# A last output transfer in three parts on two queues, and a shorter general path, in an attention and two-MoE kernel

## The chip, the cores and the metric

The kernel runs on one core of a Trainium2 chip. The metric is the time of one execution on the device in microseconds (us). TensorE is called PE, its weight loads PEld, VectorE DVE, ScalarE ACT, GpSimd POOL and SyncE SP. A profile was taken of one execution.

## The reference

Three stages follow each other; the inputs are float32 (the capacity is an integer, and some weights reach the chip as raw 64-bit words).

```python
q_p, k_p = phi(q * s), phi(k * s)          # phi: exp(h - max h) / sqrt(128), h = x @ omega.T - |x|^2 / 2
attn = (q_p @ (k_p.T @ v)) / (q_p @ k_p.sum(2) + 1e-6)      # 2 x 8 heads, 576 tokens, 64 wide
x = attn as 1152 tokens x 512
g = h * tanh(softplus(h)), h = x @ w_in                     # 512 -> 2048
x = g @ w_out                                               # 2048 -> 512
logits = x @ w_gate                                         # 8 experts
expert, gate = argmax and its softmax weight, per token
# an expert takes tokens in order up to its capacity of 288, the rest give 0
out[i] = gate[i] * (relu(x[i] @ w1[expert]) @ w2[expert])   # 512 -> 1024 -> 512
```

## The kernel before

The kernel is one function, `performer_mish_moe`, in stages: attention in 8 pairs of heads (lines 166 to 420), the first MLP's input product and its activation (lines 428 to 590), and then the routing and the experts (lines 591 to 871). The products are made in three matmuls each (`mm3`, lines 64 to 68), from a high and a low part of both operands.

The 1152 tokens form 4 groups of 288 (`G`, `GT`), each of 3 blocks of 96 (`TT`). The expert stage is written for tokens that need two pairs of a group and an expert: group 0 with its most frequent expert `eA`, and, out of groups 1 to 3, the group `g1 + 1` with its most frequent expert `eB`. These indices are found on the chip and read into registers (lines 709 to 712). The whole output is set to zero by one transfer from `zero` (line 529, pieces of 128 float32, 512 bytes), and the two pairs' results are written over it.

The second pair ends the kernel (lines 845 to 870). For each of the four 128-wide blocks `d` of the output, PE sums over 8 blocks of the hidden layer (`ffn2`). The block is copied from PSUM to `yo`, transposed on PE in three blocks of 96 tokens (`turn`), multiplied by the token's weight into `o` (`weigh`, on DVE for t = 0 and 2, on ACT for t = 1), and written to `out`. The work on block d - 1 is put into the middle of block d's sum. When blocks 0 and 1 are in `o`, SP issues their transfer (line 861, columns 0 to 255); blocks 2 and 3 go out together at the end (line 870, columns 256 to 511). Both write the rows from `row = R["g1"] * GT + GT`, a register's value, through `rows` (lines 759 and 760). In the last block the copy to `yo` is made in three pieces, all on ACT (lines 864 to 866).

```python
for t in range(3):
    c = slice(t * TT, t * TT + TT)
    S.copy(out=yo[:, 3, c], in_=py[3][:, c])
for t in range(3):
    turn(pt[t], yo, t, 3)
    weigh(o, pt[t], R["wB"], t, slice(384, 512), t == 1)
nc.sync.dma_start(out=rows(row, half[1]), in_=o[:, :, half[1]])
```

The order of instructions on each engine around here is the order of the code (`manual_schedule`); the Tile framework adds the waits on semaphores. After the last transfer every engine reads `nrem`, the number of tokens that the two pairs leave over (line 871), and branches: if it is over zero, the general path (lines 883 to 925) computes the output of all groups and experts anew. It has one loop over the 4 groups, with 16 tiles of `w_out` written out in it and 4 matmuls for each (64 in all), and a loop over groups and experts with 32 + 24 matmuls written out in it. If nothing is left over, every engine jumps over its share of this code to the end of the program, where SP and the others pass their semaphores and a common barrier.

Of the kernel before, what the change touches and what calls it, by code (L numbers as in the profile page):

```python
# [9 lines left out]
F32 = mybir.dt.float32  # L10
# [5 lines left out]
AF = mybir.ActivationFunctionType  # L16
# [4 lines left out]
NT, DM, DFF = 1152, 512, 2048  # L21
E, F1 = 8, 1024
NPAIR = NB * NH // 2
NJ = DFF // 128
KT = DM // 128
G, GT = 4, 288
TT, NTT = 96, 12
# [5 lines left out]
def performer_mish_moe(  # L33
# [15 lines left out]
    nc = tc.nc  # L49
    T, V, S, P = nc.tensor, nc.vector, nc.scalar, nc.gpsimd  # L50
# [22 lines left out]
    ident = cs[:, 0:128]  # L73
# [12 lines left out]
    def bank(tag, name):  # L86
        return psum.tile([128, 512], F32, name=name, tag=tag, bufs={"pj": 3, "qt": 2}.get(tag, 1))
# [35 lines left out]
    def convert(kind, j):  # L123

        t = raw.pop((kind, j))
        if kind == "wi":
            f = fpool.tile([128, 512], F32, name="wif", tag="wif", bufs=2)
            yield from conv64(t, f)
            yield
            hi = fhl.tile([128, KT, 128], F32R, name="wih", tag="wih")  # L130
            lo = fhl.tile([128, KT, 128], F32R, name="wil", tag="wil")
            split_hi_lo(f, hi.rearrange("p a b -> p (a b)"), lo.rearrange("p a b -> p (a b)"), "act", "dve")
            win[j] = (hi, lo)
        else:
            wo[j] = ring(F32)
            yield from conv64(t, wo[j])
# [12 lines left out]
    def steps(*gens):  # L149

        for _ in range(4):
            advance(*gens)
# [13 lines left out]
    with ExitStack() as c2:  # L166
        a1 = c2.enter_context(tc.tile_pool(name="a1", bufs=1))
# [246 lines left out]
    def g(j, c):  # L414
        return gt[j // 2][:, j % 2, c]
# [9 lines left out]
    with tc.manual_schedule():  # L425
# [97 lines left out]
        for j in range(NJ):  # L523
# [4 lines left out]
            if j == 6:  # L528
                nc.sync.dma_start(
                    out=out.rearrange("(p t) d -> p (t d)", p=128).rearrange("p (c f) -> p c f", f=128),  # L530
                    in_=zero[:, None, :].to_broadcast([128, NT * DM // 128 // 128, 128]),
                )
            if j in (9, 13):
# [3 lines left out]
                o=convert("wo", j + 1) if j + 1 < NJ else iter(()),  # L537
# [79 lines left out]
        R = {}  # L617
# [136 lines left out]
        def ffn2(n, ps, h1, f, d):  # L754
            s = slice(d * 128, d * 128 + 128)
            c = chunk[n, 8 + f]
            mm3(ps[d][:, :GT], c[0][:, s], c[1][:, s], h1[:, 0, f, :], h1[:, 1, f, :], f == 0, f == 7)

        def rows(first, c):
            return out[ds(first, GT), c].rearrange("(t p) d -> p t d", p=TT)  # L760

        def turn(pt, yo, t, d):
            T.transpose(pt[:TT, d * 128 : d * 128 + 128], yo[:, d, t * TT : t * TT + TT], ident)

        def weigh(o, pt, w, t, c, act):
            if act:
                S.activation(out=o[:, t, c], in_=pt[:TT, c], func=AF.Copy, scale=w[:, t : t + 1])
            else:
                V.tensor_scalar(out=o[:, t, c], in0=pt[:TT, c], scalar1=w[:, t : t + 1], scalar2=None, op0=ALU.mult)
# [54 lines left out]
        py = [bank(t, "py2") for t in ("b0", "b1", "b2", "qt")]  # L824
# [5 lines left out]
        yo = h3.tile([128, KT, GT], F32, name="yo", tag="em0")  # L830
# [3 lines left out]
        o = y2.tile([TT, 3, DM], F32, name="o", tag="o")  # L834
        for f in range(8):
            ffn1(1, yt1, h1, f)
            expert_split(1, 8 + f, "act", "pool" if f % 2 else "dve")
            if f < 3:
                pt = bank("pj", "pt")
# [5 lines left out]
        py = [bank(t, "py2") for t in ("b0", "b1", "b2", "qt")]  # L845
        yo = h3.tile([128, KT, GT], F32, name="yo", tag="em2")
        pt = [bank("pj", "pt") for _ in range(3)]
        o = y2.tile([TT, 3, DM], F32, name="o", tag="o")
        half = (slice(0, 256), slice(256, 512))
        row = R["g1"] * GT + GT  # L850
        for d in range(KT):
            for f in range(8):
                ffn2(1, py, h1, f, d)
                if f == 3 and d > 0:
                    for t in range(3):
                        turn(pt[t], yo, t, d - 1)
                    if d > 1:
                        for t in range(3):
                            weigh(o, pt[t], R["wB"], t, half[0] if d == 2 else slice(256, 384), t == 1)
                    if d == 2:  # L860
                        nc.sync.dma_start(out=rows(row, half[0]), in_=o[:, :, half[0]])
            if d < 3:
                (S.copy if d % 2 else V.tensor_copy)(out=yo[:, d, :], in_=py[d][:, :GT])
        for t in range(3):
            c = slice(t * TT, t * TT + TT)
            S.copy(out=yo[:, 3, c], in_=py[3][:, c])
        for t in range(3):
            turn(pt[t], yo, t, 3)
            weigh(o, pt[t], R["wB"], t, slice(384, 512), t == 1)
        nc.sync.dma_start(out=rows(row, half[1]), in_=o[:, :, half[1]])  # L870
        R["nrem"] = nc.values_load(R["ri"][0:1, 3:4], min_val=0, max_val=NT, skip_runtime_bounds_check_because="a count of tokens")
    y1.release()
    whB.release()
# [9 lines left out]
    with tc.If(R["nrem"] > 0):  # L883
        with ExitStack() as c2:
            q1 = c2.enter_context(tc.tile_pool(name="q1", bufs=1))
            q2 = c2.enter_context(tc.tile_pool(name="q2", bufs=2))
            yg = q1.tile([128, G, KT, GT], F32, name="yg")
            ob = q1.tile([TT, NTT, DM], F32, name="ob")
            V.memset(ob, 0.0)
            with tc.For_i(0, G, 1) as gi:  # L890
                ps = [bank(t, "pq") for t in ("pj", "b0", "b1", "b2")]
                for j in range(NJ):
                    t = q2.tile([128, 512], I64, name="wo64", tag="wo64")
                    nc.sync.dma_start(out=t, in_=w_out[j])
                    f = q2.tile([128, 512], F32, name="wof", tag="wof")
                    steps(conv64(t, f))
                    for d in range(KT):
                        T.matmul(out=ps[d][:, :GT], lhsT=f[:, d * 128 : d * 128 + 128], rhs=g(j, ds(gi * GT, GT)), start=(j == 0), stop=(j == NJ - 1))
                for d in range(KT):
                    V.tensor_copy(out=yg[:, ds(gi, 1), d, :].rearrange("p o t -> p (o t)"), in_=ps[d][:, :GT])  # L900
            with tc.For_i(0, G, 1) as gi:
                with tc.For_i(0, E, 1) as ei:
                    n = nc.values_load(R["cnti"][0:1, ds(gi * E + ei, 1)], min_val=0, max_val=GT, skip_runtime_bounds_check_because="a count of a group's tokens")
                    with tc.If(n > 0):
                        a1 = q1.tile([128, KT, F1], F32, name="a1", tag="a1")
                        nc.sync.dma_start(out=a1, in_=w1[ds(ei, 1)].rearrange("o (k p) f -> p (o k) f", p=128))
                        b1 = q1.tile([128, F1 // 128, DM], F32, name="b1", tag="b1")
                        nc.sync.dma_start(out=b1, in_=w2[ds(ei, 1)].rearrange("o (k p) d -> p (o k) d", p=128))
                        yc = q1.tile([128, KT, GT], F32, name="yc", tag="yc")
                        V.tensor_copy(out=yc, in_=yg[:, ds(gi, 1), :, :].rearrange("p o k t -> p (o k) t"))  # L910
                        w = q1.tile([TT, 3], F32, name="w", tag="w")
                        V.tensor_copy(out=w, in_=R["wt"][:, ds(gi * 3, 3), ds(ei, 1)].rearrange("p t e -> p (t e)"))
                        hr = q1.tile([128, 8, GT], F32, name="hr", tag="hr")
                        for f in range(8):
                            ps = bank("qt", "pq4")
                            for k in range(KT):
                                T.matmul(out=ps[:, :GT], lhsT=a1[:, k, f * 128 : f * 128 + 128], rhs=yc[:, k, :], start=(k == 0), stop=(k == KT - 1))
                            S.activation(out=hr[:, f, :], in_=ps[:, :GT], func=AF.Relu)
                        for t in range(3):
                            ps = bank("pj", "pq6")  # L920
                            for f in range(8):
                                T.matmul(out=ps[:TT, :], lhsT=hr[:, f, t * TT : t * TT + TT], rhs=b1[:, f, :], start=(f == 0), stop=(f == 7))
                            o = ob[:, ds(gi * 3 + t, 1), :].rearrange("p o d -> p (o d)")
                            V.scalar_tensor_tensor(out=o, in0=ps[:TT, :], scalar=w[:, t : t + 1], in1=o, op0=ALU.mult, op1=ALU.add)
            nc.sync.dma_start(out=out.rearrange("(t p) d -> p t d", p=TT), in_=ob)
# [64 lines left out]
```

## Time and profile before

| | us |
|---|---|
| median of 3 runs | 324.87 |
| lowest and highest of them | 324.56 to 325.56 |
| profiled execution, its own time | 324.12 |
| its span, first to last instruction | 322.3 |
| PE busy | 305.6 |
| DVE busy | 216.1 |
| ACT busy | 202.2 |
| POOL busy | 89.8 |

The profile's page gives the span, busy times and a chain of waits followed back from the last instruction. Its other views are lists of instructions in order of time, the instructions of one source line (a `q` behind an engine's name means that its sequencer ran the instruction, which does not count as busy), the waits of an engine, and the DMA queues with the packets that started in a stretch. The mean granted TensorE clock was 0.986 of full speed.

### The profile page before, as it was taken

Reading aid. Unit: us, or ns where it says so; the run is one execution under the profiler, and the core shown is the slowest. Engines: PE = TensorE matmul, PEld = TensorE weight load, DVE = VectorE, ACT = ScalarE, POOL = GpSimd, SP = SyncE. Lnnn points to the kernel's source line nnn. Section 1 sums busy time; section 2 is a strip of 40 time slices with the busy share of each in tenths; the row PEclk is TensorE's granted clock in tenths of the full one; section 3 lists DMA queues with packets and bytes.
Section 4 is the critical chain, followed back from the end, with each engine's and each line's share of the span. In section 5 each row is a group of like instructions: output and inputs, shape, how many; then the busy total and the mean of one; then the engine's idle time right before and its main releaser. Section 6 shows DMA issues by size and latency. Waiting matters only on the chain.

```text
span 322.3 us, 5943 instructions
## 1 busy us (share of the span) xinstructions
PE 305.6 (95%) x2233; PEld 276.6 (86%) x2234; DVE 216.1 (67%) x394; ACT 202.2 (63%) x385; POOL 89.8 (28%) x115
## 2 busy tenths in 40 slices
PE   8997999999999999999999999879999999999992
PEld 5885787876999899889988997749899999999991
DVE  4768899664798597977779498949844563325320
ACT  4966687864068978878697797925445662525311
POOL 1899699241000000000000011027603360423300
PEclk9997999999999999999999999979999999999998
DMA  7667743000065339825160000000224535632011
GB/s 199 248 228 262 250 132 107 2 0 2 20 231 207 132 131 317 273 97 199 64 233 29 0 2 0 1 2 1 84 81 135 163 101 192 201 96 76 1 37 43
DMA packets 18065, 36.88 MB, mean 114 GB/s; under 512 B 1552, under 2 KB 7376, under 8 KB 18032
## 3 DMA queue, kind: packets, MB, share of 16 engines
q1 hardware_dynamic: 18032, 36.45, 34.9%
q8 instruction: 19, 0.31, 0.4%
q14 instruction: 14, 0.11, 0.1%
HBM read 32.91 MB, written 3.54 MB: 113 GB/s over the span
## 4 chain that ended last, share of the span: by engine, by line
PE 73%; DVE 11%; ACT 7%; DMA 3%; issue 3%; SPq 1%; POOL 0%; DVEq 0%; ACTq 0%; POOLq 0%
PE h L66 9%; PE h L67 9%; PE h L68 9%; PE py L67 5%; PE py L68 5%; PE py L66 5%; PE kvp L250 3%; DVE gh L62 3%; PE num L283 3%; PE lg L487 2%; PE ph L66 2%; PE ph L67 2%; PE ph L68 2%; PE pj L66 2%; PE pj L68 2%
## 5 line engine op out<-in xcount | busy, mean ns | idle before, releaser
L62 POOL TENSOR_TENSOR wl<-wl,whi 128x512 fp32r<-128x512 f32 x28 | 37.6, 1351 | 192.5 <-ACT em L477 117.8
L66 PE MATMUL h<-xh,wih 128*128 128x384 f32 x192 | 66.5, 346 | 0.5 <-DVE g L431 0.5
L67 PE MATMUL h<-xl,wih 128*128 128x384 f32 x192 | 64.4, 336 | 0.0
L68 PE MATMUL h<-xh,wil 128*128 128x384 f32 x192 | 64.4, 336 | 0.0
L66 PEld LDWEIGHTS h<-xh,wih 128*128 128x128 f32 x192 | 36.1, 188 | 5.0 <-issue 2.9
L67 PE MATMUL py<-gh,whi 128*128 128x288 f32 x128 | 38.2, 299 | 0.9 <-DVE gh L62 0.8
L66 PE MATMUL py<-gh,whi 128*128 128x288 f32 x128 | 38.4, 300 | 0.0
L68 PE MATMUL py<-gh,wl 128*128 128x288 f32 x128 | 37.7, 294 | 0.0
L67 PEld LDWEIGHTS h<-xl,wih 128*128 128x128 f32 x192 | 36.1, 188 | 0.5 <-issue 0.5
L68 PEld LDWEIGHTS h<-xh,wil 128*128 128x128 f32 x192 | 36.0, 188 | 0.0
L231 DVE TENSOR_REDUCE nm<-pj 128x4 f32<-128x512 f32 x36 | 24.4, 688 | 11.2 <-PE pj L68 10.9
L62 DVE TENSOR_TENSOR gh<-g,gh 128x288 fp32r<-128x288 f32 x32 | 22.5, 712 | 13.8 <-ACT gh L56 13.7
L238 ACT ACTIVATE e<-pj,nm 128x128 f32<-128x128 f32 x72 | 22.5, 377 | 14.1 <-DVE e L236 7.4
L481 DVE TENSOR_TENSOR g<-g,em 128x1152 f32<-128x1152 f32 x16 | 21.6, 1357 | 13.4 <-ACT em L479 13.3
L56 ACT CAST whi<-wl 128x512 fp32r<-128x512 f32 x43 | 25.4, 616 | 2.1 <-DVE sm L668 1.1
L67 PEld LDWEIGHTS py<-gh,whi 128*128 128x128 f32 x128 | 24.2, 189 | 1.8 <-DVE gh L62 1.8
L66 PEld LDWEIGHTS py<-gh,whi 128*128 128x128 f32 x128 | 24.0, 188 | 1.6 <-DVE gh L62 0.8
L62 POOL TENSOR_TENSOR kql<-kqf,kqh 128x256 fp32r<-128x256 f32 (+2 forms) x29 | 23.3, 824 | 7.3 <-ACT kqh L56 7.1
L68 PEld LDWEIGHTS py<-gh,wl 128*128 128x128 f32 x128 | 24.1, 189 | 0.0
L66 PE MATMUL pj<-omh,kqh 128*128 128x256 f32 x72 | 23.1, 321 | 0.0
L62 DVE TENSOR_TENSOR wl<-wl,whi 128x512 fp32r<-128x512 f32 x20 | 16.9, 845 | 8.6 <-PE py L68 3.6
L431 DVE COPY g<-h 128x384 f32<-128x384 f32 x36 | 19.9, 552 | 4.2 <-PE h L68 4.2
(150 smaller groups left out, 734.8 us busy)
## 6 DMA issues: line engine op xcount, KB each, us to landing
wi<-w_in SPq DMA_DIRECT2D x16, 512.0 KB, 3.6
wo<-w_out SPq DMA_DIRECT2D x16, 512.0 KB, 4.3
wl<-w SPq DMA_DIRECT2D x32, 256.0 KB, 2.9
out<-zero SPq DMA_DIRECT2D x1, 2304.0 KB, 11.7
kqf<-kq SPq DMA_DIRECT2D x3, 640.0 KB, 4.0
v<-va SPq DMA_DIRECT2D x4, 390.0 KB, 4.2
kqf<-kq SPq DMA_DIRECT2D x3, 512.0 KB, 4.9
v<-va SPq DMA_DIRECT2D x4, 260.0 KB, 5.3
```

What stands on the lines that cost most here:

```text
L56: S.copy(out=hi, in_=src)
L62: e.tensor_tensor(out=lo, in0=src, in1=hi.bitcast(F32), op=ALU.subtract)
L66: T.matmul(out=o, lhsT=lh, rhs=rh, start=start, stop=False)
L67: T.matmul(out=o, lhsT=lh, rhs=rl, start=False, stop=False)
L68: T.matmul(out=o, lhsT=ll, rhs=rh, start=False, stop=stop)
L231: V.tensor_reduce(out=nm, in_=pv, op=ALU.max, axis=AX.X, negate=True)
L238: S.activation(out=e[:, j, :], in_=pv[:, j, :], func=AF.Exp, bias=nm[:, j : j + 1])
L250: T.matmul(out=K[:, c : c + 65], lhsT=e[t][:, h, :], rhs=v[:, (2 * t + h) * 65 : (2 * t + h + 1) * 65], start=(p % 2 == 0 and h == 0 and t ...
L283: T.matmul(out=o[32 * i : 32 * i + 32, :GT], lhsT=d[w][:, h, r, s], rhs=d["qT"][:, r, h, c * GT : c * GT + GT], start=True, stop=True, til ...
L431: (S.copy if c == 2 and j < 12 else V.tensor_copy)(out=g(j, slice(c * 384, c * 384 + 384)), in_=ps)
L481: V.tensor_tensor(out=hv, in0=hv, in1=em.pop(j), op=ALU.mult)
L487: T.matmul(out=lg[c][i * 32 : i * 32 + 32, :], lhsT=wg[:, j, :], rhs=g(j, slice(c * 384, c * 384 + 384)), start=(b == 0), stop=(b == 3), t ...
```

## The change

Three things change. In block d = 3 of the last sum, once block 2 is in `o`, a transfer of its own writes columns 256 to 383, so that the end has columns 384 to 511 alone; these go out in two transfers, t = 1 on ACT's queue and t = 0 and 2 on SP's. The three copies to `yo` of the last block go to DVE, ACT and DVE. And the general path is written with fewer instructions: its first loop goes over 12 blocks of 96 tokens with 16 matmuls and 4 transposes in it, and the 32 matmuls of its second part are a loop over 8 with 4 in it, with `w1` loaded in pieces; that leaves 16 + 4 + 4 + 24 = 48 PE operations in the code.

```diff
                     if d > 1:
                         for t in range(3):
                             weigh(o, pt[t], R["wB"], t, half[0] if d == 2 else slice(256, 384), t == 1)
-                    if d == 2:
-                        nc.sync.dma_start(out=rows(row, half[0]), in_=o[:, :, half[0]])
+                    if d > 1:
+                        c = half[0] if d == 2 else slice(256, 384)
+                        nc.sync.dma_start(out=rows(row, c), in_=o[:, :, c])
             if d < 3:
                 (S.copy if d % 2 else V.tensor_copy)(out=yo[:, d, :], in_=py[d][:, :GT])
         for t in range(3):
             c = slice(t * TT, t * TT + TT)
-            S.copy(out=yo[:, 3, c], in_=py[3][:, c])
+            (S.copy if t == 1 else V.tensor_copy)(out=yo[:, 3, c], in_=py[3][:, c])
+        c = slice(384, 512)
         for t in range(3):
             turn(pt[t], yo, t, 3)
-            weigh(o, pt[t], R["wB"], t, slice(384, 512), t == 1)
-        nc.sync.dma_start(out=rows(row, half[1]), in_=o[:, :, half[1]])
+            weigh(o, pt[t], R["wB"], t, c, t == 1)
+        nc.scalar.dma_start(out=rows(row, c)[:, 1:2], in_=o[:, 1:2, c])
+        nc.sync.dma_start(out=rows(row, c)[:, 0:3:2], in_=o[:, 0:3:2, c])
...
-            with tc.For_i(0, G, 1) as gi:
-                ps = [bank(t, "pq") for t in ("pj", "b0", "b1", "b2")]
+            with tc.For_i(0, NTT, 1) as ti:
+                gj = q1.tile([128, NJ, TT], F32, name="gj", tag="gj")
+                for j in range(NJ):
+                    V.tensor_copy(out=gj[:, j, :], in_=g(j, ds(ti * TT, TT)))
+                ps = bank("pj", "pq")
                 for j in range(NJ):
...
-                    for d in range(KT):
-                        T.matmul(out=ps[d][:, :GT], lhsT=f[:, d * 128 : d * 128 + 128], rhs=g(j, ds(gi * GT, GT)), start=(j == 0), stop=(j == NJ - 1))
+                    T.matmul(out=ps[:TT, :], lhsT=gj[:, j, :], rhs=f, start=(j == 0), stop=(j == NJ - 1))
+                yd = q1.tile([TT, DM], F32, name="yd", tag="yd")
+                V.tensor_copy(out=yd, in_=ps[:TT, :])
+                pt = bank("b0", "pq2")
                 for d in range(KT):
-                    V.tensor_copy(out=yg[:, ds(gi, 1), d, :].rearrange("p o t -> p (o t)"), in_=ps[d][:, :GT])
+                    T.transpose(pt[:, d * TT : d * TT + TT], yd[:, d * 128 : d * 128 + 128], ident[:TT, :TT])
+                V.tensor_copy(out=yg[:, ds(ti, 1), :, :].rearrange("p o k t -> p (o k t)"), in_=pt[:, 0 : KT * TT])
...
-                        for f in range(8):
+                        with tc.For_i(0, 8, 1) as fi:
+                            a1 = q1.tile([128, KT, 128], F32, name="a1", tag="a1")
+                            nc.sync.dma_start(out=a1, in_=w1[ds(ei, 1), :, ds(fi * 128, 128)].rearrange("o (k p) f -> p (o k) f", p=128))
                             ps = bank("qt", "pq4")
                             for k in range(KT):
-                                T.matmul(out=ps[:, :GT], lhsT=a1[:, k, f * 128 : f * 128 + 128], rhs=yc[:, k, :], start=(k == 0), stop=(k == KT - 1))
+                                T.matmul(out=ps[:, :GT], lhsT=a1[:, k, :], rhs=yc[:, k, :, :].rearrange("p t c -> p (t c)"), start=(k == 0), stop=(k == KT - 1))
```

## Rows read from the trace of the kernel before

**Rows 1.** The page: the span, and busy time of each engine.
```profile
span 322.3 us, 5943 instructions
...
PE 305.6 (95%) x2233; PEld 276.6 (86%) x2234; DVE 216.1 (67%) x394; ACT 202.2 (63%) x385; POOL 89.8 (28%) x115
```

**Rows 2.** The chain of waits, 314 to 323 us: start, length, what.
```profile
315.95 0.63 DVE o L769 x2
```

**Rows 3.** Instructions in order of time near the end: start, length, engine, line, operation.
```profile
309.98 0.87 DVE L769 TENSOR_SCALAR o<-pt,wB 96x256 f32<-96x256 f32 x2 [4.77 <-PE pt L763]
...
310.97 0.35 SPq L861 DMA_DIRECT2D out<-o  x1
...
313.49 0.60 DVE L769 TENSOR_SCALAR o<-pt,wB 96x128 f32<-96x128 f32 x2 [1.25 <-PE pt L763]
...
315.30 0.52 ACT L866 COPY yo<-py 128x96 f32<-128x96 f32 x3 [1.34 <-PE py L68]
...
315.60 0.60 PE L763 MATMUL pt<-cs,yo 128*96 128x128 f32 x3 [0.33 <-ACT yo L866]
315.95 0.63 DVE L769 TENSOR_SCALAR o<-pt,wB 96x128 f32<-96x128 f32 x2 [1.85 <-PE pt L763]
316.09 0.36 ACT L767 ACTIVATE o<-pt,wB 96x128 f32<-96x128 f32 x1 [0.26 <-PE pt L763]
316.72 0.32 SPq L870 DMA_DIRECT2D out<-o  x1
```

**Rows 4.** Line L883: durations in ns (least/median/most), first and last start.
```profile
L883 ACTq COMPARE_BRANCH  x1: 50/50/50, 316.4 to 316.4; - x1
L883 PEldq COMPARE_BRANCH  x1: 3982/3982/3982, 316.5 to 316.5; - x1
L883 DVEq COMPARE_BRANCH  x1: 72/72/72, 316.6 to 316.6; - x1
...
L883 SPq EVENT_SEMAPHORE  x3: 17/17/17, 317.9 to 318.1; - x3
...
L883 SPq EVENT_SEMAPHORE  x4: 17/17/17, 320.6 to 320.8; - x4
```

**Rows 5.** Line L986, the closing barrier, in the same columns.
```profile
L986 PEldq DRAIN  x1: 8/8/8, 320.8 to 320.8; - x1
...
L986 SPq DRAIN  x2: 7/10/13, 321.5 to 321.6; - x2
```

**Rows 6.** Issue to landing in us: L861, then L870; then issues by size.
```profile
DMA to landing us min/median/max: 2.7/2.7/2.7
...
DMA to landing us min/median/max: 3.9/3.9/3.9
...
out<-zero SPq DMA_DIRECT2D x1, 2304.0 KB, 11.7
...
out<-o SPq DMA_DIRECT2D x1, 576.0 KB, 3.7
```

**Rows 7.** DMA from 317 to 320: busy tenths in 40 slices; instruction fetches; then 317.6 to 317.7.
```profile
DMA  0000000399988898699997244210211020111100
...
q8 instruction: 1, 0.02, 2.3%
...
q8 instruction: 1, 0.02, 68.4%
```

**Rows 8.** SP's waits: who waited for whom, us in total, times, longest.
```profile
SPq L737 <- PE py L68: 15.6, 9, 5.0
...
SPq L737 <- DVE wl L62: 8.7, 8, 1.5
...
SPq L737 <- POOL wl L62: 3.0, 3, 1.7
...
SPq L870 <- DMA out<-o: 2.2, 1, 2.2
```

**Rows 9.** Instructions of a line of the general path, whole span.
```profile
nothing on L925; most used: ['L66', 'L67', 'L68', 'L283', 'L250', 'L62', 'L487', 'L56', 'L442', 'L271', 'L737', 'L238', 'L448', 'L120', 'L431', 'L763', 'L58', 'L241', 'L231', 'L986', 'L252', 'L109', 'L111', 'L113', 'L456']
```

More of the change, by code (lines that the diff above doesn't have):

```diff
@@ L886, in performer_mish_moe @@
             q2 = c2.enter_context(tc.tile_pool(name="q2", bufs=2))
-            yg = q1.tile([128, G, KT, GT], F32, name="yg")
+            yg = q1.tile([128, NTT, KT, TT], F32, name="yg")
             ob = q1.tile([TT, NTT, DM], F32, name="ob")
             V.memset(ob, 0.0)
-            with tc.For_i(0, G, 1) as gi:
-                ps = [bank(t, "pq") for t in ("pj", "b0", "b1", "b2")]
+            with tc.For_i(0, NTT, 1) as ti:
[3 more added lines that the diff above has]
+                ps = bank("pj", "pq")
                 for j in range(NJ):
@@ L904, in performer_mish_moe @@
                     with tc.If(n > 0):
-                        a1 = q1.tile([128, KT, F1], F32, name="a1", tag="a1")
-                        nc.sync.dma_start(out=a1, in_=w1[ds(ei, 1)].rearrange("o (k p) f -> p (o k) f", p=128))
                         b1 = q1.tile([128, F1 // 128, DM], F32, name="b1", tag="b1")
                         nc.sync.dma_start(out=b1, in_=w2[ds(ei, 1)].rearrange("o (k p) d -> p (o k) d", p=128))
-                        yc = q1.tile([128, KT, GT], F32, name="yc", tag="yc")
-                        V.tensor_copy(out=yc, in_=yg[:, ds(gi, 1), :, :].rearrange("p o k t -> p (o k) t"))
+                        yc = q1.tile([128, KT, 3, TT], F32, name="yc", tag="yc")
+                        for t in range(3):
+                            V.tensor_copy(out=yc[:, :, t, :], in_=yg[:, ds(gi * 3 + t, 1), :, :].rearrange("p o k t -> p (o k) t"))
                         w = q1.tile([TT, 3], F32, name="w", tag="w")
@@ L913, in performer_mish_moe @@
                         hr = q1.tile([128, 8, GT], F32, name="hr", tag="hr")
-                        for f in range(8):
+                        with tc.For_i(0, 8, 1) as fi:
+                            a1 = q1.tile([128, KT, 128], F32, name="a1", tag="a1")
+                            nc.sync.dma_start(out=a1, in_=w1[ds(ei, 1), :, ds(fi * 128, 128)].rearrange("o (k p) f -> p (o k) f", p=128))
                             ps = bank("qt", "pq4")
                             for k in range(KT):
-                                T.matmul(out=ps[:, :GT], lhsT=a1[:, k, f * 128 : f * 128 + 128], rhs=yc[:, k, :], start=(k == 0), stop=(k == KT - 1))
-                            S.activation(out=hr[:, f, :], in_=ps[:, :GT], func=AF.Relu)
+                                T.matmul(out=ps[:, :GT], lhsT=a1[:, k, :], rhs=yc[:, k, :, :].rearrange("p t c -> p (t c)"), start=(k == 0), stop=(k == KT - 1))
+                            S.activation(out=hr[:, ds(fi, 1), :].rearrange("p o t -> p (o t)"), in_=ps[:, :GT], func=AF.Relu)
                         for t in range(3):
```

## The prediction

> **What bounds the kernel now.** I read the page first. PE is busy for 305.6 of the 322.3 us [rows 1], so before the last output only PE time could be won, and the change touches none there. Then the chain of waits: its last piece is the two last multiplications on DVE, over at 315.95 + 0.63 = 316.58 [rows 2]. The chain stops there, 5.7 us before the span does, because what follows is the work of sequencers and DMA, which that view doesn't follow.
>
> So I read those 5.7 us by line. Three things happen in them.
> - SP issues the last transfer (L870) at 316.72, 0.14 us after DVE's end [rows 3]. It lands after 3.9 us [rows 6], at 320.6.
> - Every engine branches over the general path (L883), which doesn't run: none of its lines is in the trace [rows 9]. ACT takes 50 ns for the branch, DVE 72, PE 3982 [rows 4]. PE therefore comes to the closing barrier only at 320.8 [rows 5].
> - SP goes through one semaphore after the other. Three are done by 318.1, the next is passed at 320.6, and from there it goes by steps of 0.07 [rows 4]. That stop ends when L870's transfer lands. SP reaches the barrier at 321.5 to 321.6 [rows 5], 0.7 us after PE, and the span ends at 322.3 [rows 1].
>
> **The last transfer sets the end.** 1.7 us of fixed steps follow its landing, and PE's slow branch is hidden with 0.7 us to spare.
>
> Why does it take 3.9 us, when L861, of the same shape and size, takes 2.7 [rows 6]? In 317 to 320 a 16 KB instruction fetch (q8) holds 2.3% of 16 engines' 3 us, which is 1.1 us of one DMA engine. The DMA line falls from 9 to 2, 1 and 0 tenths (one engine of 16 is 0.06) and lasts into 320.1 [rows 7]: one or two engines finish late. So a fetch across a transfer costs 3.9 - 2.7 = 1.2 us.
>
> **The change, part by part.**
>
> *Copies of yo.* Three ACT copies (0.52 us in all, from 315.30) become two on DVE and one on ACT. Transposes still go in the order 0, 1, 2. Two DVE operations on 128 columns took 0.60 us together [rows 3], so two on 96 take at most that, and the first about 0.3; before, the first ACT copy released PE at 315.60. I add 0.06 us (0 to 0.1): ACT's last multiplication ends at 316.09 + 0.36 + 0.06 = 316.5, DVE's at 316.64.
>
> *Splitting by columns.* Columns 256 to 383 leave early: DVE is done with them at 313.49 + 0.60 = 314.09. After L861's analogous step (309.98 + 0.87 = 310.85, issue at 310.97) I add 0.12, which gives an issue at 314.21 [rows 3]. SP only waits there, so nothing queues behind it.
>
> *Landing times of smaller pieces.* 576 KB took 3.7 and 288 KB 2.7 [rows 6], so 1.0 us per 288 KB on 1.7 us. The new pieces are 512 bytes long, as those of `zero` are: 2304 KB in 11.7 us, so (11.7 - 1.7) / 2304 = 0.0043 us per KB. By this, 144 KB land in 2.3 us, 96 KB in 2.1 and 48 KB in 1.9. The bounds are the first slope (2.2, 2.0, 1.9) below and L861's 2.7 above.
>
> *A wait between the parts.* This decides. Before L870's transfer, SP waited 2.2 us for DMA `out<-o` [rows 8], which is L861's: issued at 310.97, landed at 313.7. Both only read `o`, in different columns, and both write `out` at the same row, read from a register, again in different columns. So two writes of `out` at a row known only at run time are put one after the other even where their columns are disjoint. The 32 expert loads (L737), whose address is also read at run time, wait for PE, DVE and POOL, and that view has no wait of theirs for a landing [rows 8]: it is the writes that are ordered. Before, this wait cost nothing, as it ended 3 us ahead of the data. Now three transfers stand behind L861, each at a run-time row, so each waits for the one ahead:
> 1. SP, columns 256 to 383: issue 314.21, landing 314.21 + 2.3 = 316.5.
> 2. ACT, t = 1: its data are there at 316.5, the landing too. With SP's 0.14 it issues at 316.65. No transfer issued by ACT is in the trace; nearest is SP's. Below that I see nothing; above, I allow 0.4 for its registers. Landing 316.65 + 1.9 = 318.55. Behind it on ACT stand only the load of nrem and the branch, which have until 321.
> 3. SP, t = 0 and 2: the data are there at 316.64, but it waits for ACT's landing: issue 318.55 + 0.14 = 318.7, landing + 2.1 = 320.8. The load of nrem, the branch and the first semaphores, over 1.4 us after the issue before (316.72 to 318.1), fit in that.
>
> So the landing moves from 320.6 to 320.8: + 0.2. Two more transfers put the last one's semaphore two places further along in SP's row, which saves 2 x 0.07: - 0.13. Sum: + 0.07, a span of 322.4.
>
> Of two queues the trace shows only what an issue costs, 0.32 us on SP at L870 [rows 3]. The Trainium skill, "DMA: Bandwidth & Descriptors", section "Issuing engines are not separate DMA queues", says that transfers from several engines run on the same 16 DMA engines and that several issuers save the issuing time alone. By that rule the second queue is worth 0.3 us at most, even without any wait. No run here shows it.
>
> *48 matmuls for 120.* None runs. What shrinks is the code that PE skips. If its branch becomes like DVE's, PE is at the barrier before 318, and nothing comes of it while SP is last.
>
> The profiled execution took 324.12 us, 1.8 around its span of 322.3; the median of the runs is 324.87. On the median's scale + 0.07 is 324.94, rounded to **325.0**. By ACT's issue and the landing bounds it lies in 324.4 to 325.7. A measurement of this kernel tells 0.3% (0.97 us) from no change.
>
> **The rivals.**
> - *Slower: a fetch across a chained transfer.* PE's branch began at 316.5 [rows 4], and the 16 KB fetch between 317.6 and 317.7 [rows 7]. ACT's transfer runs in 317.5 to 318.5, just there. If one engine has its pieces behind the fetch, ACT's landing is up to 1.2 us late, and SP's transfer is late by as much: + 1.3, 326.2. For it: that happened to L870. Against it: ACT's pieces are a sixth of L870's bytes and may be through already, and PE may no longer fetch at that point. It decides from a delay of 0.9 us on.
> - *Faster: no wait between the parts.* Should the framework see that t = 1 and t = 0, 2 don't overlap, both are issued by 316.8. Together they are 144 KB on the same engines, landing by 316.8 + 2.3 = 319.1: - 1.5, and - 0.13, so 323.2. That holds only if PE's branch is short and its fetch misses the transfer. Against it: L870 waited though its columns were disjoint.
> - *The code on PE stays too long.* The branch still takes 4 us and PE comes at 320.8. Chained, that changes nothing. Without the chain it is a floor: SP's arrival can move from 321.55 to 320.8 only, - 0.75, so 324.1. Against it: half of the matmuls and more are gone, and the branches of ACT and DVE are short. The Trainium skill, "Runtime: NRT & Kernel Launch", section "Instruction fetch mechanics", says that a taken branch to a page outside the two held waits for a DMA fetch. The trace agrees for PE (3982 ns, a 16 KB fetch); by that rule this rival needs a path still longer than those pages.
>
> **How the numbers follow.** Chained without a collision 0.54, chained with one 0.22, no wait 0.18, no wait but a long branch 0.06. Slower by over 0.3%: 0.18 of the second case (the rest delays less) and 0.02 of the first, 0.20. Faster: 0.17 of the third and 0.02 of the others, 0.19. Same: the remaining 0.61. The range reaches up to the collision, 326.2, and down to 323.8, which leaves out most of the no-wait case (0.15) and little else.
>
> **What would show it.** Right: on SP a wait of about 2 us for ACT's transfer ahead of the last issue; an issue near 318.7; the last landing near 320.8; PE's branch well under 1 us. Wrong: SP's last issue near 316.8 (the chain doesn't exist), a landing later than 321.3 (a collision), or a PE branch near 4 us. Any shift before 313 us would mean that I missed an effect altogether.

## The result, and the profile after

The changed kernel took 327.14 us (median of 9 runs, 325.29 to 328.12), the kernel before 324.62 (9 runs, 324.02 to 325.56). The ratio is 1.0097 [1.0071, 1.0124]: **slower by 2.5 us**. The forecast was 325.0 in a range of 323.8 to 326.2, so the time lies outside it, on the side of the first rival and beyond it.

The page of the changed kernel opens with the span and the busy times [rows 1], and part 3 of it (packets, MB, share) has a queue that was not there, ACT's.

```profile
span 325.2 us, 5952 instructions
...
PE 306.7 (94%) x2233; PEld 277.9 (85%) x2234; DVE 217.7 (67%) x396; ACT 201.9 (62%) x383; POOL 89.8 (28%) x115
...
q10 hardware_dynamic: 112, 0.05, 0.1%
```

The profiled execution took 327.14 us, as long as the median. Its last matmul of the expert sums (L68) starts at 315.26, in the trace of before at 314.97. From there to the end of the span I call **the tail**: 7.33 us before, 9.95 after. A tail is read from one execution; of the kernels below that were run twice, the two tails differ by at most 0.17 us. The tail is 2.62 longer and holds the whole loss.

Instructions in order of time near the end, after [rows 3]; columns as there.

```profile
314.53 0.32 SPq L862 DMA_DIRECT2D out<-o  x1
...
315.26 0.29 PE L68 MATMUL py<-h,wl 128*128 128x288 f32 x1
315.59 0.26 DVE L867 COPY yo<-py 128x96 f32<-128x96 f32 x1 [1.20 <-PE py L68]
315.88 0.24 ACT L867 COPY yo<-py 128x96 f32<-128x96 f32 x1 [1.63 <-DVE yo L867]
...
316.16 0.26 DVE L867 COPY yo<-py 128x96 f32<-128x96 f32 x1 [0.31 <-ACT yo L867]
...
316.53 0.36 ACT L767 ACTIVATE o<-pt,wB 96x128 f32<-96x128 f32 x1 [0.41 <-PE pt L763]
316.82 0.35 DVE L769 TENSOR_SCALAR o<-pt,wB 96x128 f32<-96x128 f32 x1 [0.15 <-PE pt L763]
316.92 0.40 ACTq L872 DMA_DIRECT2D out<-o  x1
320.67 0.32 SPq L873 DMA_DIRECT2D out<-o  x1
```

Two things are to be seen. The three copies come one after the other, each waiting for the one ahead on the other engine; the last multiplication ends at 317.17, which is 1.91 after the start of the last L68, where before it was 1.61. And SP's data are there at 317.17, but its transfer is issued at 320.67. What it waits for stands in SP's waits [rows 8]:

```profile
SPq L873 <- DMA out<-o: 5.5, 1, 5.5
...
SPq L862 <- DMA out<-o: 2.2, 1, 2.2
```

The first line is ACT's transfer. It lands 3.56 us after its issue, and SP's own takes 2.94. Issue to landing [rows 6], lines L862, L872 and L873:

```profile
DMA to landing us min/median/max: 2.0/2.0/2.0
...
DMA to landing us min/median/max: 3.6/3.6/3.6
...
DMA to landing us min/median/max: 2.9/2.9/2.9
```

So 144 KB took 2.0 us, and then a third of them took 3.6. The DMA view shows why [rows 7]. First 316.8 to 324 (each slice is 0.18 us), then 318.6 to 320.2 alone:

```profile
DMA  0000019110100010000000000098500100000000
...
q8 instruction: 2, 0.03, 2.1%
q14 instruction: 3, 0.02, 1.3%
...
DMA  0000800000000000001010201000000000000000
...
q10 hardware_dynamic: 7, 0.00, 2.1%
```

Both transfers are a short block of high digits with thin 1s behind it; some of the 1s are instruction fetches (rows q8 and q14), the last ones are late pieces. ACT's 112 packets are through by 318.2, all but seven, and these go out one at a time between 319.3 and 319.8: the share of one DMA engine. PE's 16 KB fetch began at 318.01 and took 1.35, so it ended at 319.37, just where they begin. An 8 KB fetch (q14) ends there too, at 319.35, so this transfer alone doesn't tell the two apart. The next one does: of SP's transfer the late pieces begin at 322.58, where PE's next 16 KB fetch ends, while an 8 KB fetch is still running (322.46 to 322.85). The trace doesn't name the DMA engine of a packet; that fetch and late pieces share one is read from these times. The trace has a completion of each of the 16 DMA engines: 15 came within 1.61 us of ACT's issue, the last after 3.56. Of SP's transfer 15 came within 1.75 us, the last after 2.94; across it lies that next 16 KB fetch, which began at 321.49 and took 1.10.

The branch over the general path, now L886 [rows 4], and the closing barrier, now L997 [rows 5]:

```profile
L886 SPq EVENT_SEMAPHORE  x9: 17/17/17, 321.9 to 323.8; - x9
...
L886 PEldq COMPARE_BRANCH  x1: 3742/3742/3742, 317.1 to 317.1; - x1
L886 DVEq COMPARE_BRANCH  x1: 72/72/72, 317.2 to 317.2; - x1
L886 ACTq COMPARE_BRANCH  x1: 54/54/54, 317.7 to 317.7; - x1
...
L997 SPq DRAIN  x3: 7/7/13, 324.4 to 324.7; - x3
...
L997 PEldq DRAIN  x2: 8/8/8, 321.2 to 324.8; - x2
```

PE's branch still takes 3.7 us, with 44 matmuls and 4 transposes in place of 120 matmuls. PE is at the barrier at 321.2 and waits there 3.3 us for SP.

The tail, step by step (us). "No path" is experiment e7 below, the changed kernel without the general path; the forecast's column is worked from the prediction's times, 314.97 being the start of the last L68:

| | before | forecast | after | no path (e7) |
|---|---|---|---|---|
| last L68 to the issue on ACT (before: on SP) | 1.75 | 1.68 | 1.66 | 1.66 |
| its landing | 3.86 | 1.9 | 3.56 | 1.61 |
| to the issue on SP | - | 0.15 | 0.19 | 0.19 |
| its landing | - | 2.1 | 2.94 | 1.74 |
| to the end of the span | 1.73 | 1.60 | 1.60 | 1.07 |
| sum | 7.3 | 7.4 | 9.95 | 6.26 |

Against the forecast the two landings are 1.66 and 0.84 longer, 2.50 together. Every other step is within 0.04.

### The profile page after: what moved, and what is told of

Its sections match the earlier page's. It is cut to its first block, busy times and chain, and to the rows that moved or that the text cites. A ratio compares the mean times of both kernels' runs of the same rounds, so it can differ in the third digit from the quotient of the medians.

```text
span 325.2 us, 5952 instructions
## 1 busy us (share of the span) xinstructions
PE 306.7 (94%) x2233; PEld 277.9 (85%) x2234; DVE 217.7 (67%) x396; ACT 201.9 (62%) x383; POOL 89.8 (28%) x115
## 4 chain that ended last, share of the span: by engine, by line
PE 71%; DVE 10%; ACT 7%; DMA 4%; issue 3%; POOL 2%; SPq 0%; DVEq 0%; ACTq 0%; POOLq 0%
PE h L66 9%; PE h L67 9%; PE h L68 9%; PE py L66 6%; PE py L67 6%; PE py L68 6%; PE kvp L250 3%; PE num L283 3%; DVE gh L62 3%; DMA kqf<-kq 2%; PE lg L487 2%; PE ph L66 2%; PE ph L68 2%; PE ph L67 2%; PE wt L442 2%
## 5 line engine op out<-in xcount | busy, mean ns | idle before, releaser
L68 PE MATMUL h<-xh,wil 128*128 128x384 f32 x192 | 64.4, 336 | 0.0
L68 PE MATMUL py<-gh,wl 128*128 128x288 f32 x128 | 37.7, 294 | 0.0
L68 PEld LDWEIGHTS h<-xh,wil 128*128 128x128 f32 x192 | 36.0, 188 | 0.0
L68 PEld LDWEIGHTS py<-gh,wl 128*128 128x128 f32 x128 | 24.3, 190 | 0.0
```

The lines of the kernel that those rows point to most:

```text
L68: T.matmul(out=o, lhsT=ll, rhs=rh, start=False, stop=stop)
```

## The experiments

Each ratio is to the kernel before, run beside it on the same chip. Where no ratio moves, the tail is the sharper measure.

### The two halves of the change

**e1** is the kernel before with the change's copies and transfers, **e2** the kernel before with the change's general path:

```diff
e1, against the changed kernel
-            with tc.For_i(0, NTT, 1) as ti:
+            with tc.For_i(0, G, 1) as gi:
...
e2, against the changed kernel
-        nc.scalar.dma_start(out=rows(row, c)[:, 1:2], in_=o[:, 1:2, c])
-        nc.sync.dma_start(out=rows(row, c)[:, 0:3:2], in_=o[:, 0:3:2, c])
+        nc.sync.dma_start(out=rows(row, half[1]), in_=o[:, :, half[1]])
...
```

> The three transfers and the copies of the change, with the general path of before. Theory A (chain: each write of out waits for the landing of the one ahead, and an instruction fetch of PE lies across the last two): all of the loss is here, 327.1 us, 2.5 above before. Theory B (the shorter general path moves code and fetches and costs time itself): 324.6 to 325.2.

> The general path of the change with the last transfer of before. Theory A: within 0.3 us of before (324.6), since SP and not PE comes last to the barrier. Theory B: 326 to 327.1. PE's branch shows whether its cost hangs on the length skipped: by the prediction under 1 us, by the trace of the change about 3.7 us still.

e1 took 327.19 us, ratio 1.0098 [1.0064, 1.0132], tail 10.23: ACT's 48 KB landed after 3.13, SP's 96 KB after 3.65. e2 took 324.53, 1.0019 [0.9988, 1.0051], tail 7.92; its 288 KB landed after 4.3. All of the loss comes with the transfers and copies. The shorter path brings nothing, and does not even shorten PE's branch (e2, line L883):

```profile
L883 PEldq COMPARE_BRANCH  x1: 4378/4378/4378, 316.4 to 316.4; - x1
```

### The wait between the parts

**e3** gives the row as a constant (576, what the register holds for these inputs), so that the framework can see that the three writes don't overlap:

```diff
-        row = R["g1"] * GT + GT
+        row = 576
```

> The changed kernel with the row of the second pair's transfers written as 576, its value with these inputs, in place of a register: the framework then sees that the parts don't overlap and sets no wait between them. Theory A: both last transfers are issued by 317.3 and land by 319 without a fetch across them, by 320.5 with one: 323.4 to 325.0 us. Theory C (the copies to yo that wait for one another, not the chain, cost the time): 326.5 to 327.1.

It took 323.96 us, ratio 0.9997 [0.9962, 1.0032], tail 7.22: 2.7 less than the changed kernel. In the view of SP's waits L873 waits for its data and no longer for ACT's transfer:

```profile
SPq L873 <- DVE o L769: 2.3, 1, 2.3
```

Both are issued within 0.27 us (instructions in order of time):

```profile
317.15 0.39 ACTq L872 DMA_DIRECT2D out<-o  x1
317.42 0.32 SPq L873 DMA_DIRECT2D out<-o  x1
```

And the DMA view of 317 to 321.5:

```profile
q8 instruction: 1, 0.02, 2.2%
...
out<-o SPq DMA_DIRECT2D x1, 96.0 KB, 3.7
out<-o ACTq DMA_DIRECT2D x1, 48.0 KB, 3.8
```

The wait is what the register's row brings. The last view shows the rest: one 16 KB fetch (318.21 to 319.80) lies across both transfers, and each lands after 3.7 to 3.8. The late pieces of ACT's transfer go out from 319.77 to 320.18 and those of SP's right behind them, to 320.58, so both transfers share one delay, where the chain pays for two. (The 8 KB fetches had ended by 319.66.) So without the wait the change is worth nothing over before, not a gain.

### The copies

**e4** is the changed kernel with its three copies on ACT, as before:

```diff
-            (S.copy if t == 1 else V.tensor_copy)(out=yo[:, 3, c], in_=py[3][:, c])
+            S.copy(out=yo[:, 3, c], in_=py[3][:, c])
```

> The changed kernel with all three last copies to yo on ACT as before. Theory C: ACT and DVE no longer wait for each other, the last multiplication ends 0.3 to 0.6 us earlier and the time falls to 326.5 to 326.8 at most. If the copies cost 2 us by what follows them, 325. Theory A: 326.5 to 327.1, for the chain of landings stays.

It took 326.95 us, 1.0111 [1.0065, 1.0158], tail 9.79. The last multiplication ends 1.61 after the last L68 again, 0.30 earlier than in the changed kernel, but the tail is only 0.16 shorter: the copies' 0.30 is real and is mostly hidden behind the wait for ACT's transfer. Against the kernel before e4 loses as much as the change does.

### Without the general path

These leave out the general path, which doesn't run for these inputs: **e6** from the kernel before, **e7** from the changed one. **e9** is the kernel before with a path that only writes zeros, so that the branch stays and PE has next to nothing to skip.

```diff
-    with tc.If(R["nrem"] > 0):
...
-            nc.sync.dma_start(out=out.rearrange("(t p) d -> p t d", p=TT), in_=ob)
```

> The kernel before without the general path and its branch (nothing of the result with these inputs depends on it). Theory D (the fetch that PE's branch causes lies across the last transfer and makes one of 16 DMA engines late): no fetch near the end, the transfer lands 2.7 us after its issue in place of 3.9, the time falls by 1.0 to 1.5 us. Theory E (a transfer at the very end lands late by itself): landing 3.9 us still, the time within 0.4 us of before.

> The changed kernel without the general path and its branch. Theory D: the chain stays, but each of its two last transfers lands 1.6 to 1.8 us after its issue; by the copies' 0.3 to 0.5 us the time is 0 to 0.8 us over the kernel before with its path, 2 to 3 us under the changed kernel. Theory E: 326.5 to 327.1.

> The kernel before with a general path that only writes zeros (it leaves out the computation for left-over tokens, of which these inputs have none), so that PE has next to nothing to jump over. If the length skipped decides PE's branch: under 0.5 us, no 16 KB fetch about 1 us behind it, and the time 1.0 to 1.5 us under before. If any taken branch of PE at this place costs a fetch: about 4 us, and the time within 0.4 us of before.

| | us | ratio to before | tail |
|---|---|---|---|
| e6 | 323.47 | 0.9951 [0.9924, 0.9977] | 5.58 |
| e7 | 323.37 | 0.9969 [0.9942, 0.9995] | 6.26 |
| e9 | 323.40 | 0.9969 [0.9941, 0.9997] | 5.60 |

The three DMA views of the end have no row for q8 or q14 at all, and the transfers land when their last pieces should. e6, the 288 KB in 317.9 to 320.7; then e7, 317.5 to 321.2:

```profile
q1 hardware_dynamic: 304, 0.29, 39.2%
...
out<-o SPq DMA_DIRECT2D x1, 288.0 KB, 2.6
```

```profile
DMA  0000000000188300000000000000058997200000
...
q1 hardware_dynamic: 208, 0.10, 11.1%
q10 hardware_dynamic: 112, 0.05, 5.7%
...
out<-o SPq DMA_DIRECT2D x1, 96.0 KB, 1.7
out<-o ACTq DMA_DIRECT2D x1, 48.0 KB, 1.6
```

In e7 the chain is still there (SP waits 3.6 us for ACT's transfer), the two blocks have no thin 1s behind them, and the tail is 3.7 shorter than in the changed kernel. **The chain alone costs little; the chain with a late DMA engine in each of its links does not.** Without the path the changed kernel's tail is 0.68 us over that of the kernel before (6.26 against 5.58, the slower copies included), with it 2.62. And the kernel before had been paying for late engines all along (two of its 16 completions came after 3.62 and 3.86 us, the others within 2.59): 7.33 - 5.58 = 1.75 us of tail, of which 1.2 is the landing. e7 came out better than expected, 1.0 us below the kernel before by its ratio and not 0 to 0.8 us over it; 0.5 us of that is in the steps behind the landing (1.07 for 1.60).

### One last transfer in place of two

**e5** keeps the early transfer of columns 256 to 383, has its copies on ACT, and sends the last 144 KB in one transfer on SP; **e5b** is the same kernel again.

```diff
-        nc.scalar.dma_start(out=rows(row, c)[:, 1:2], in_=o[:, 1:2, c])
-        nc.sync.dma_start(out=rows(row, c)[:, 0:3:2], in_=o[:, 0:3:2, c])
+        nc.sync.dma_start(out=rows(row, c), in_=o[:, :, c])
```

> The changed kernel with the copies on ACT and one last transfer of columns 384 to 511 on SP, so split by columns alone. Issue at 316.7 as before, 15 of 16 engines done 2.0 us later, the late one by 320.3 to 321: without a chain the time is within 0.6 us of before, 2 to 3 us under the changed kernel. If the division between queues isn't what costs: 326.5 to 327.1.

> The kernel e5_one_last_transfer again, beside the two above on one chip: PE's branch about 4 us, one DMA engine late, within 0.6 us of before.

e5's 12 runs have a median of 324.26 us (before 324.3); the ratio that came with it, 0.9858, rests on two of them alone (318.22 and 321.73), so e5b decides. It took 324.14, 1.0018 [0.9987, 1.0048], tail 6.94 (e5: 7.10). Halving the last transfer wins 0.2 to 0.4 of tail and not 0.65, what 288 against 144 KB would give (2.65 - 2.00): 14 DMA engines were done 1.98 us after e5's issue, the last two after 2.99 and 3.57.

### How much code PE jumps over

By a count in the compiled programs, which no trace here shows, this many PE instructions stand behind the branch, where a float32 matmul counts as two weight loads and two matmuls (the trace shows 128 records of each for the 64 matmuls of line 250): 637 before, 298 in the changed kernel. **e10** is e5 with the three blocks of 96 tokens as a loop, **e11** also has the 16 tiles of `w_out` in a loop:

```diff
-                        for t in range(3):
+                        with tc.For_i(0, 3, 1) as ti:
...
-                for j in range(NJ):
+                with tc.For_i(0, NJ, 1) as ji:
```

> The same with the 24 matmuls alone in a loop, about 255 instructions to jump over. Theory F: at the limit, short or long, and the time goes with it: 1.8 to 2.4 us under before or within 0.6 us of it. Theory G: 4 us, within 0.6 us.

> Split by columns alone (one last transfer on SP, copies on ACT) with the 24 and the 16 written-out matmuls of the general path in loops too, so that PE has about 217 instructions to jump over in place of 298 in the change and 637 before (a float32 matmul counted as two matmuls and two weight loads, as the trace shows them). Theory F (the branch is short if the target lies in the page that PE holds besides the current one; PE is near a page's end at the branch, so about 256 are the limit): branch under 0.5 us, no fetch near the last transfer, landing 2.0 us after its issue, 1.8 to 2.4 us under before. Theory G (any long skip costs the fetch): branch 4 us, the time within 0.6 us of before.

> e11_217_to_skip with the general path taken always: it computes every group and expert anew. By far slower than all others (no theory hangs on it).

| instructions PE skips | 637 (before, e1) | 298 (e2, after) | 255 (e10) | 217 (e11) | 1 (e9) |
|---|---|---|---|---|---|
| PE's branch, us | 3.98, 3.32 | 4.38, 3.74 | 0.35 | 0.36 | 0.22 |

e3, e4, e5 and e5b, also with 298, lie between 3.78 and 3.96. e10 took 324.79, 1.0043 [1.0019, 1.0068], tail 7.29; e11 323.67, 0.9999 [0.9972, 1.0026], tail 6.70. The branch is short, PE is at the barrier at 318.0 in e11, and nothing comes of it, as the prediction said of a short branch. For the fetch is still there: in e11 it begins at 318.44, 1.1 us after the start of PE's branch, takes 1.41, and the 144 KB issued at 317.56 land after 3.5 (the DMA view of 317.5 to 321.1):

```profile
q8 instruction: 1, 0.02, 2.4%
...
out<-o SPq DMA_DIRECT2D x1, 144.0 KB, 3.5
```

Stall and collision are two things, so neither theory came out whole: F was right on the branch, G on the time of e11. e10 fits neither: by its ratio it is 0.4% slower than the kernel before, though its tail is 0.04 us shorter. Its loss isn't explained here, and a ratio so near to 1 says little without a tail that agrees. With the condition forced to be true, **e12** ran e11's path: one run of 2480.39 us, so the path costs some 2157 us when it is needed. What the path of the kernel before costs then was not measured.

### When the fetch comes

**e13** is e11 with PE held back before its branch by work that nothing uses: a DVE multiplication of 128x1152 and a transpose that reads it. So the fetch starts later. **e14** has the same hold and path with the last transfer of the kernel before. **e13b** and **e14b** are the same two kernels again.

```diff
+        dly = h3.tile([128, KT * GT], F32, name="dly", tag="em0")
+        yf = yo.rearrange("p k t -> p (k t)")
+        V.tensor_tensor(out=dly, in0=yf, in1=yf, op=ALU.mult)
+        T.transpose(bank("b0", "dm")[:TT, 0:128], dly[:, 0:TT], ident)
         R["nrem"] = nc.values_load(R["ri"][0:1, 3:4], min_val=0, max_val=NT, skip_runtime_bounds_check_because="a count of tokens")
```

> e11_217_to_skip with PE held back at the end: DVE does a product of 128x1152 elements after its last multiplication (about 1.4 us by L481's rows), and PE transposes a part of it before it reads nrem and branches. Theory D (the late DMA engine is the fetch that follows PE's branch by about 1 us, whatever the branch itself takes): the fetch comes after the last transfer's packets, which lands 2.0 us after its issue in place of 3.5; 1.0 to 2.0 us under before. Theory E (the end of the program makes one engine late in another way): landing 3.5 us still, within 0.6 us of before.

> The same hold and the same general path with the last transfer of before (columns 256 to 511 in one). Theory D: landing 2.7 us after its issue; 0.5 to 1.3 us under before, and 0.6 us over e13_fetch_later, which is what the split by columns is worth when nothing lies across it.

> The same kernel as e13. Theory (one engine's pieces late behind an instruction fetch that PE's branch starts): again a landing of 2.0 to 2.3 us after the last issue, PE's 16 KB fetch starting after the landing, and a ratio below 1, 0.993 to 0.999. Rival (the gain of e13 was chance, which 8 KB fetch meets which transfer changes from run to run): a landing of 3 us or more, and a ratio of 1.000.

> The same kernel as e14, whose one traced transfer was late by 1 us with PE's 16 KB fetch out of the way. Theory a (the 8 KB fetches of the other engines alone suffice to make one engine's share of a 288 KB transfer late, every time): landing 3.5 us or more again, ratio 0.997 to 1.001. Theory b (they seldom do; only the 16 KB fetch does so every time): landing 2.6 to 2.9, and a ratio near 0.995.

| | us | ratio to before | tail | landing of the last transfer |
|---|---|---|---|---|
| e13 | 323.12 | 0.9962 [0.9930, 0.9995] | 5.63 | 2.24 |
| e13b | 322.78 | 0.9961 [0.9930, 0.9992] | 5.70 | 2.24 |
| e14 | 324.45 | 0.9986 [0.9955, 1.0018] | 6.91 | 3.65 |
| e14b | 323.96 | 0.9984 [0.9956, 1.0011] | 6.91 | 3.66 |

**e13 beats the kernel before, twice**: by 0.4%, with a tail 1.6 to 1.7 us (0.5%) shorter. By the quotient of the ratios it is 1.3% ahead of the changed kernel (0.9962 / 1.0097 = 0.9866). In the trace of e13b PE branches at 319.5:

```profile
L889 PEldq COMPARE_BRANCH  x1: 353/353/353, 319.5 to 319.5; - x1
```

Its 16 KB fetch begins at 320.61, after the landing at 319.94, so the DMA view of 317.71 to 319.95 has no q8 row:

```profile
q1 hardware_dynamic: 304, 0.15, 27.4%
q14 instruction: 3, 0.02, 3.4%
...
out<-o SPq DMA_DIRECT2D x1, 144.0 KB, 2.2
```

e13 against e11 is the cleanest test of the 16 KB fetch: in both, three 8 KB fetches lie across the same 144 KB, and with PE's fetch after the landing it lands after 2.24 us in place of 3.5.

e14 does not fit so simply. PE's fetch comes late there as well, and still 288 KB land as late as ever, twice. Three 8 KB fetches lie across them. In e14b all pieces of the transfer are through by 318.52, except two packets: two 8 KB fetches run from 318.12 to 318.55 and from 318.51 to 318.82, and the last two packets go out from 318.82 to 318.88. The DMA view from 318.52 to 320 (0.037 us a slice) shows those and the 16 KB fetch alone:

```profile
DMA  0000000000000000000000090000000000000000
...
q8 instruction: 1, 0.02, 4.1%
q1 hardware_dynamic: 2, 0.00, 0.3%
```

15 engines complete within 2.62 us, the last at 3.66, that is 1.0 us after its last packet; in the other transfers of these runs that step is 0.3 to 0.8. The packets are 0.36 us late, behind the 8 KB fetches; the rest of the delay is in the completion. PE's 16 KB fetch is not quite out of the way: it begins at 319.41, after the last packet but 0.50 us before the landing, in e14 0.49 before it. With a completion 0.46 us after the last packet, as in the kernel before, e14b's landing would have come at 319.34 (an estimate), before that fetch began. So whether the 8 KB fetches did it all, as one theory for e14b had it, or the start of the 16 KB fetch drew out the completion, stays open. In e13b, where PE's fetch begins 0.66 us after the landing, three 8 KB fetches across the 144 KB cost 0.24 at most (2.24 against 2.00).

## Why the prediction was wrong

- **What sets the end** was right: the last transfer. SP reaches the barrier 3.3 us after PE.
- **The early column split** was right: issue at 314.53, which is 314.24 on the scale of before (0.29 off for the later body), where 314.21 was forecast.
- **The wait between writes at a run-time row** was right, and it decided: SP waits for ACT's transfer (5.5 us on L873, of which the data account for some 2.2), and with a constant row it doesn't (e3). The rival without a wait was wrong.
- **The landing times without a fetch** were each some 0.3 too long: 2.0, 1.61 and 1.74 (L862 and e7) for 2.3, 1.9 and 2.1. That erred towards slow and hid a part of the collisions: they cost 3.14 us, and the two landings of the chain, together 0.64 too long in the forecast, took the miss down to 2.50.
- **The copies** were mis-sized: + 0.06 (0 to 0.1) was forecast; against the last L68 DVE's end came 0.30 later, and ACT's start of t = 1 0.15 later (316.53 - 315.26 = 1.27, before 316.09 - 314.97 = 1.12). The step assumed that copies on two engines take no longer than three on ACT. They went strictly in turn (0.26, 0.24, 0.26 with 0.03 between), while ACT's three had overlapped to 0.52 [rows 3]. Which of the two shared tiles, `py` or `yo`, makes the wait was not tried. The chain hid most of it (e4).
- **The code on PE**: "If its branch becomes like DVE's" failed. The third rival's premise, that the code stays too long, came true: 298 instructions, and the branch took 3.7 us. The prediction counted 48 PE operations and never what each becomes. The Trainium skill, "Runtime: NRT & Kernel Launch", section "Instruction fetch mechanics", speaks of blocks of 16 KB with 256 instructions. The short branches at 217 and 255 and the long ones at 298 and 637 agree with a reach of about one block ahead, as far as four lengths can show it; where in its block the branch stands was not varied.
- **The step that failed** is the pair of landings taken without a collision, 1.9 and 2.1. They measured 3.56 and 2.94. The rival "a fetch across a chained transfer" had the mechanism and its place, and was given 0.22 and + 1.3; it happened, to both links, for 1.95 (3.56 - 1.61, its other 15 engines) and 1.19 (2.94 - 1.75). Two readings would have shown it:
  - The base held one collision in its 3.86, and the forecast took it out of the changed kernel for two reasons. That PE may no longer fetch at that point failed twice: the branch stayed long, and e10 and e11 had a short branch, the fetch and the late landing. That ACT's pieces are few and may be through already held for 15 DMA engines of 16, and a transfer lands with the last.
  - The trace of before has a second 16 KB fetch, at 321.14, 0.69 us after the end of PE's branch (316.47 + 3.98 = 320.45). It cost nothing there, since L870 had landed at 320.57. After: 317.06 + 3.74 = 320.80, and 0.69 later the fetch begins, at 321.49. By then the chain had moved SP's issue to 320.67, so it fell across the new last transfer. This second collision the prediction had not seen. It also contradicts the third rival's "Chained, that changes nothing": this second fetch is in every trace with a long branch, and in none with a short one.
- **The second queue** was weighed with 0.3 us at most. ACT's issue took 0.40, SP's 0.32. Without the wait, two queues (e3, tail 7.22, of which up to 0.3 is the copies) are no better than one (e5, e5b: 7.10, 6.94). That agrees with the rule that the prediction quoted from the Trainium skill, "DMA: Bandwidth & Descriptors", section "Issuing engines are not separate DMA queues": the same DMA engines serve both. So does e3, where the late pieces of SP follow those of ACT behind one fetch.
- **Two semaphores further along** were to save 0.13 after the landing: 1.60 against 1.73. The size is right, but the reason isn't shown, and luck may be in it: with one transfer more than before e5 and e5b took 1.80, and the step lies between 1.46 and 2.05 in the kernels that jump over a path that computes.

So the mechanism of the loss is the chain times the fetches: e3 keeps the fetches and drops the chain, e7 keeps the chain and drops the fetches, and each alone brings the time back to that of before or below.

## What to carry to other kernels

A transfer is as late as its slowest DMA engine (here 15 done after 1.61 us, the last after 3.56): where the last landing sets the end, look at what else the DMA engines carry in that stretch, instruction fetches included, and at what the base already pays for it. Dividing a last write into parts that the framework must order, such as parts at a row known only at run time, multiplies that cost by the number of links, so keep the last write whole. Code that never runs still costs when it is jumped over at the end. A shorter jump alone brought nothing here (e10, e11); what helped was next to nothing to jump over (e9), or a fetch that starts after the last landing (e13).

## What the runs showed that was not expected

- PE's branch shows a step and no slope over the five lengths tried: 0.35 us with 255 instructions to skip, 3.7 to 4.4 with 298, 3.3 to 4.0 with 637.
- A branch of 0.35 us is still followed by a 16 KB fetch 1.1 to 1.2 us after its start (e10, e11, e13, e14). Only with next to nothing to skip (e9) is there none.
- A 288 KB transfer with 8 KB fetches (0.3 to 0.6 us each) across its packets and the start of a 16 KB one across its completion landed 1.0 us late, the same to 0.01 us in two runs (e14, e14b: 3.65, 3.66). Which of them costs what is open.
- Small writes land soon when nothing is in the way: 48 KB in 1.61, 96 KB in 1.74, 144 KB in 2.00, 288 KB in 2.65 us.
- Copies of one tile on DVE and ACT went in turn, 0.03 us apart, and on two engines the three took longer (0.83, from 315.59 to 316.42) than on one (0.52).
